# Lo parts of weights and V from GpSimd to VectorE, and the softmax's small scalings from ScalarE to GpSimd

## The chip, the cores and the metric

The kernel runs on one core of one Trainium2 chip. The core has TensorE (PE; its weight loads are listed apart as PEld), VectorE (DVE), ScalarE (ACT), GpSimd (POOL) and SyncE (SP, which here only issues DMAs). Each engine works through its own queue in order, and semaphores let one wait for another. The metric is the device time of one execution in microseconds (us); lower is better. Times of the kernel before are the median of three runs, and one more execution was recorded by the hardware profiler.

## The reference

Attention with a mask from hashing, followed by a feed-forward layer with ELU. Cut to what matters:

```python
# q, k, v: (4, 8, 768, 64); proj: (64, 6); w_in: (512, 2048); w_out: (2048, 512), all float32
q_bits = einsum('bhsd,dk->bhsk', q, proj) > 0      # 6 bits: a bucket per row
k_bits = einsum('bhsd,dk->bhsk', k, proj) > 0
mask = q_bucket[..., :, None] == k_bucket[..., None, :]
scores = where(mask, q @ k.T / sqrt(64), -1e9)
scores -= scores.max(-1)
attn = exp(scores)
attn = attn / (attn.sum(-1) + 1e-9)
x = (attn @ v), heads beside each other            # (3072, 512)
h = x @ w_in
g = where(h > 0, h, exp(min(h, 0)) - 1)
out = g @ w_out                                    # (3072, 512)
```

## The kernel before

**Numbers as two halves.** Matmuls run in f16. To keep precision each f32 operand is scaled by a power of two and split: the hi part is the scaled value rounded to f16, the lo part is the scaled value less the hi part, again in f16. A product is then three matmuls: hi by hi, hi by lo, lo by hi. The helper `scaled` makes a hi part, `rest` a lo part; each takes a `kind` and looks in the table ENGINES for the engine. An entry has two strings, the first for the time until all weights are decoded (`now[0]` is 0), the second for the time after; several letters in a string are used in turn. A is ScalarE, V is VectorE, G is GpSimd. For V, `rest` is one instruction on VectorE (L151, scalar_tensor_tensor: x times s, less hi). For G it is two on GpSimd: x times s in place (L153), then less hi (L154).

**Attention.** A batch has 8 heads in 4 pairs, and its 768 rows are cut into two chunks of three tiles of 128, so there are 8 chunks. A slot is one tile of rows of one head; 24 slots make a chunk, 192 the whole. In a slot PE computes the scores of 128 rows against 768 keys into a bank pair of PSUM (L556). The mask is part of this product: the bits are further rows of its operands. DVE copies the scores to SBUF as `pt` and takes each row's maximum into `m` (L568). Two slots make a duo. For a duo, `exps` multiplies the two columns of maxima by the row's factor into `nb` (L581), and ACT takes the exponentials with `nb` as bias and gives the row sums `sm` (L584). One slot later `splits` makes `r` from `sm`: times 2^-14, plus a small constant (L593), and DVE takes the reciprocal (L594). Then ACT makes the hi part of the duo's two `pt` tiles (L142, hl), DVE the lo part (L151, hl), and SP issues a DMA that transposes both into PT (L599). The product with V (`attend`, L607) follows AV_LAG = 4 slots after a pair's last slot and gives x16 in two halves (L616 on ACT, L617 on DVE).

**Preparation.** K and Q of coming pairs are loaded, scaled, split and transposed ahead of their slots. V of a batch is split by `prep_v`: its hi parts on ACT, its lo parts in 8 pieces of 128x384 per batch. For the first batch this happens while weights are still being decoded.

**Weights.** w_in and w_out come as 16 blocks of 128x512 each. Their f32 values are rebuilt from the two halves in which they are loaded: L516 on ACT, L517 and L518 on DVE; PE sums their squares (L526). Once a matrix's scale is known, `wsplit` makes a block's hi part on ACT (L142, W) and its lo part by `rest`. A block group (4 blocks of w_in, 4 of w_out) must be split before the feed-forward part reaches it (`need_w`).

**Feed-forward (MoE in the code).** It begins after slot 30 with chunk 0 and then runs beside the attention of later chunks. For each of 16 column blocks: 12 matmuls give h (L636); ACT takes the exponential (L647); POOL multiplies and adds (L650); DVE takes a maximum and a minimum (L651); ACT and DVE make hi and lo parts of g (L142 and L151, U); PE adds to the output banks (L672). At a chunk's end ACT and DVE empty three output banks and POOL issues the output DMA for each (L686).

**Order.** A planner sets the order within each engine's queue: it takes the program's order as priority and places what is ready by its own timing of the instructions. From the slot where the feed-forward part begins, PE's order is that of the program. An instruction that the planner put in a queue keeps the ones behind it waiting when its inputs are late.

Of the kernel before, what the change touches and what calls it, by code (L numbers as in the profile page):

```python
# [13 lines left out]
AF = mybir.ActivationFunctionType  # L14
ALU = mybir.AluOpType
# [7 lines left out]
P_TOP = 14  # L23
# [28 lines left out]
    "n_hi": ("A", "A"),  # L52
    "n_lo": ("V", "V"),
    "v_hi": ("A", "A"),
    "v_lo": ("G", "V"),
    "w_hi": ("A", "A"),
    "w_lo": ("G", "G"),
    "g_hi": ("A", "A"),
    "g_lo": ("V", "V"),
    "dup": ("V", "V"),  # L60
# [5 lines left out]
def lsh_attention_moe(  # L66
# [10 lines left out]
    nc = tc.nc  # L77
# [60 lines left out]
    def scaled(kind, o, x, s):  # L138

        e = engine(kind)  # L140
        if e == "A":
            nc.scalar.activation(o, x, AF.Copy, scale=s)  # L142
        elif e == "V":
            nc.vector.tensor_scalar(o, x, s, None, ALU.mult)
        else:
            nc.gpsimd.tensor_scalar(o, x, s, 1.0, ALU.mult, ALU.mult)

    def rest(kind, o, x, s, hi):

        if engine(kind) == "V":  # L150
            nc.vector.scalar_tensor_tensor(o, x, s, hi, ALU.mult, ALU.subtract)  # L151
        else:
            nc.gpsimd.tensor_scalar(x, x, s, 1.0, ALU.mult, ALU.mult)  # L153
            nc.gpsimd.tensor_tensor(o, x, hi, ALU.subtract)  # L154
# [421 lines left out]
    def exps(st, duo):  # L576

        m, pts = duo[0], duo[1:]
        w = len(pts)
        nb = small.tile([P, 2], F32, tag="nb", name="nb")  # L580
        nc.scalar.activation(nb[:, :w], m[:, :w], AF.Copy, scale=st["sg"][:, 1:2])  # L581
        sm = small.tile([P, 2], F32, tag="sm", name="sm")
        for n, pt in enumerate(pts):
            nc.scalar.activation(  # L584
                pt, pt, AF.Exp, bias=nb[:, n : n + 1], scale=st["sg"][:, 0:1], accum_out=sm[:, n : n + 1]
            )
        return sm, pts

    def splits(sm, pts, PTs):

        w = len(pts)
        r = small.tile([P, 2], F32, tag="r", name="r")
        nc.scalar.activation(r[:, :w], sm[:, :w], AF.Copy, scale=2.0**-P_TOP, bias=1e-9 * 2.0**-P_TOP)  # L593
        nc.vector.reciprocal(r[:, :w], r[:, :w])  # L594
        for n, pt in enumerate(pts):
            hl = pp.tile([P, 2, S], F16, tag="p", name="hl")
            scaled("p_hi", hl[:, 0, :], pt, r[:, n : n + 1])
            rest("p_lo", hl[:, 1, :], pt, r[:, n : n + 1], hl[:, 0, :])
            nc.sync.dma_start_transpose(PTs[n].rearrange("p x c e -> p (x c) e"), hl.rearrange("p x e -> p (x e)"))  # L599
# [189 lines left out]
    for ns in groups:  # L789
# [3 lines left out]
        for n in ns:  # L793
            at = lead[2] if early else begin[n] - PREP[2]

            w = 2 * chunks[pairs[n][0]]["nc"]
# [144 lines left out]
    def run_splits():  # L941
        if behind:
            splits(*behind.pop())

    for G in range(starts[-2] + 1):
        if G == starts[0]:
            ordered.enter_context(tc.manual_schedule(engines={mybir.EngineType.PE}))
        if G < len(slots):
            n, at = slots[G]
            c = chunks[pairs[n][0]]  # L950
            b, p, j, t = c["b"], pairs[n][1], at // c["nc"], at % c["nc"]
            now[0] = int(w_at == NSI + NSO)
            if t == 0:
                (PT,) = pt_ring.take(c["nc"], pairs[n][0])
                PTs = PTs + [PT] if j else [PT]
            if G < starts[0] and G % 2:
                s_tile = ps_o.tile([P, 2, 512], F32, tag="o", name="so")
            else:
                s_tile = ps_s.tile([P, 2, 512], F32, tag="s", name="s")
            scores(ks[b, p], qs[n], at, j, s_tile, duo, G >= starts[0])  # L960
            into.append(PT[:, t])

            run_splits()
            if len(into) == 2:
                behind.append((*exps(qs[n], duo), into))
                duo, into = [], []
            if at == 2 * c["nc"] - 1:
                assert not into
                waiting.append((G + AV_LAG, (n, PTs)))
        else:  # L970
            run_splits()
# [39 lines left out]
```

## Time and profile before

| | |
|---|---|
| median of 3 runs | 927.86 us (924.74 to 927.88) |
| profiled execution, its own time | 925.77 us |
| its span in the profile | 923.3 us |
| mean granted PE clock | 0.938 |
| GpSimd L650, L154, L153 | 128, 40 and 40 instructions |
| DMA moved | 135.11 MB, mean 146 GB/s |

The page of the profile gives each engine's busy time and its share of the span, and, for the costliest groups, a line of the kernel, engine, operation, the tiles written and read, shapes, the count, then busy us and mean ns of one; behind the last bar stands how long the engine sat idle just before them and what ended that. A row of waits reads: engine and line that waited, what it waited for, us in total, times, longest us. A row of one line's or tile's instructions gives minimum, median and maximum of the duration in ns, then the first and last start in us.

### The profile page before, as it was taken

The page shows a single profiled execution, that of the slowest core. Times are in us where ns is not written, and L with a number is a line of the kernel's source. Part 1 is how long each engine was busy: PE and PEld are TensorE (multiplying, and loading weights), DVE is VectorE, ACT ScalarE, POOL GpSimd, SP SyncE. Part 2 cuts the span into 40 slices and gives each one's busy share as a digit, 9 for nine tenths or more (in the row PEclk, how much of TensorE's full clock was granted, in tenths as well). Part 3 has the DMA queues.
Part 4 walks back from the last instruction along what each step waited for, and adds up shares of the span by engine and source line. Part 5 has one row for each costly group of instructions (what it writes and reads, how often), then busy time and mean ns, then how long its engine had stood idle before and what let it go on. Part 6 is the DMA issues. An engine that isn't in the chain of part 4 may idle for free.

```text
span 923.3 us, 14935 instructions
## 1 busy us (share of the span) xinstructions
PE 823.7 (89%) x5161; PEld 434.4 (47%) x5161; DVE 698.3 (76%) x1490; ACT 696.0 (75%) x1361; POOL 221.9 (24%) x259
## 2 busy tenths in 40 slices
PE   4475745899999999999989999999999999999996
PEld 2232312455545555555545555555445555555553
DVE  6999968788878778788868687889878687674332
ACT  7876878989869677789879677888687777774322
POOL 1703579631112011212211111221111112111211
PEclk9577656899999999999999999999999999999998
DMA  9799576798787857698897776896876678554000
GB/s 327 202 282 254 143 148 128 138 170 174 154 177 160 144 111 142 146 191 141 154 216 130 129 127 120 165 192 110 158 140 130 118 118 151 100 108 84 35 1 34
DMA packets 391338, 135.11 MB, mean 146 GB/s; under 512 B 368000, under 2 KB 385632, under 8 KB 391264
## 3 DMA queue, kind: packets, MB, share of 16 engines
q1 hardware_dynamic: 389184, 127.88, 69.3%
q0 software_dynamic: 1920, 6.29, 2.0%
q8 instruction: 40, 0.66, 0.3%
q14 instruction: 34, 0.28, 0.1%
q10 hardware_dynamic: 160, 0.00, 0.0%
HBM read 35.65 MB, written 6.29 MB: 45 GB/s over the span
## 4 chain that ended last, share of the span: by engine, by line
PE 45%; DVE 19%; DMA 13%; ACT 12%; issue 8%; POOL 1%; SPq 1%; ACTq 0%; POOLq 0%; DVEq 0%
PE h L636 16%; PE o L672 15%; PE s L556 7%; PE av L607 6%; DVE pt L568 5%; DVE hl L151 4%; DMA K<-natk 4%; ACT pt L584 3%; DMA O<-nat1q 3%; ACT hl L142 3%; DMA PT<-hl 2%; DMA out_dram<-W 2%; DVE W L518 1%; ACT U L647 1%; PE z L315 1%
## 5 line engine op out<-in xcount | busy, mean ns | idle before, releaser
L672 PE MATMUL o<-W,U 128*128 128x512 f16 x1152 | 280.9, 380 | 2.4 <-ACT W L142 2.4
L636 PE MATMUL h<-x,W 128*128 128x384 f16 x1536 | 280.5, 327 | 2.6 <-DVE x L617 2.2
L650 POOL TENSOR_SCALAR U<-U,ch 128x384 f32<-128x384 f32 x128 | 113.4, 886 | 572.1 <-ACT U L647 506.0
L636 PEld LDWEIGHTS <-W 128*128 128x128 f16 x1536 | 147.5, 98 | 114.1 <-issue 10.7
L151 DVE SCALAR_TENSOR_TENSOR hl<-pt,r,hl 128x768 f16<-128x768 f32 x192 | 193.9, 1038 | 6.3 <-ACT hl L142 5.9
L584 ACT ACTIVATE pt<-pt,nb,sg 128x768 f32<-128x768 f32 x192 | 195.3, 1018 | 2.2
L142 ACT ACTIVATE hl<-pt,r 128x768 f16<-128x768 f32 x192 | 168.4, 925 | 29.8 <-DVE r L594 27.6
L568 DVE TENSOR_SCALAR_CACHE_REDUCE pt<-s 128x768 f32<-128x768 f32 x177 | 168.0, 949 | 25.1 <-PE s L556 24.4
L556 PE MATMUL s<-K,O 128*128 128x384 f16 x708 | 151.5, 337 | 22.7 <-DVE pt L568 19.8
L672 PEld LDWEIGHTS <-U 128*128 128x128 f16 x1152 | 111.1, 98 | 122.3 <-issue 8.8
L556 PEld LDWEIGHTS <-O 128*128 128x128 f16 (+1 forms) x768 | 74.8, 102 | 115.6 <-issue 59.2
L651 DVE SCALAR_TENSOR_TENSOR U<-h,U 128x384 f32<-128x384 f32 x128 | 70.8, 553 | 74.8 <-POOL U L650 74.7
L647 ACT ACTIVATE U<-h,ch 128x384 f32<-128x384 f32 x128 | 72.8, 569 | 66.2 <-PE h L636 66.1
L607 PE MATMUL av<-PT,vhl 128*64 128x384 f16 x1152 | 106.9, 332 | 3.8 <-DMA PT<-hl 3.7
L151 DVE SCALAR_TENSOR_TENSOR U<-U,ch 128x384 f16<-128x384 f32 x128 | 79.6, 623 | 39.7 <-ACT U L142 39.4
L142 ACT ACTIVATE U<-U,ch 128x384 f16<-128x384 f32 x128 | 77.2, 605 | 40.8 <-DVE U L651 40.5
L607 PEld LDWEIGHTS <-vhl 128*64 128x64 f16 x1152 | 68.8, 111 | 44.4 <-issue 15.4
L154 POOL TENSOR_TENSOR W<-W 128x512 f16<-128x512 f32 x32 | 43.5, 1363 | 2.2
L581 ACT ACTIVATE nb<-m,sg 128x2 f32<-128x2 f32 x96 | 27.5, 287 | 16.4 <-DVE pt L568 15.9
L584 ACT ACTIVATION_READ_ACCUMULATOR pt<-pt,nb,sg 128x1 f32 x192 | 36.0, 187 | 0.0
L526 PE MATMUL acc<-W 128*128 128x128 bf16 x128 | 17.8, 283 | 19.7 <-DVE W L518 19.2
L556 PE MATMUL so<-K,O 128*128 128x384 f16 (+1 forms) x60 | 18.7, 449 | 17.9 <-DVE pt L568 16.6
(126 smaller groups left out, 632.5 us busy)
## 6 DMA issues: line engine op xcount, KB each, us to landing
U<-in_moe_w_in_dram SPq DMA_DIRECT2D x12, 512.0 KB
vf<-in_v_dram SPq DMA_DIRECT2D x16, 384.0 KB
U<-in_moe_w_out_dram SPq DMA_DIRECT2D x12, 512.0 KB
out_dram<-W POOLq DMA_DIRECT2D x24, 256.0 KB, 3.4
qst<-in_q_dram SPq DMA_DIRECT2D x30, 192.0 KB
kst<-in_k_dram SPq DMA_DIRECT2D x14, 384.0 KB
PT<-hl SPq DMA_TRANSPOSE x192
W<-in_moe_w_in_dram SPq DMA_DIRECT2D x4, 512.0 KB
```

Of the source, the lines that this page charges most:

```text
L142: nc.scalar.activation(o, x, AF.Copy, scale=s)
L151: nc.vector.scalar_tensor_tensor(o, x, s, hi, ALU.mult, ALU.subtract)
L154: nc.gpsimd.tensor_tensor(o, x, hi, ALU.subtract)
L556: nc.tensor.matmul(s_tile[:, n, :HALF], st[o][:rows, at, :], kst[kk][:rows, j * NC + n * HC : j * NC + (n + 1) * HC, :].rearrange("p a b - ...
L568: top = nc.vector.tensor_scalar(pt.rearrange("p (n e) -> p n e", n=2), s_tile[:, :, :HALF], CLAMP, None, ALU.max, ALU.max, accum_out=duo[0 ...
L584: nc.scalar.activation(pt, pt, AF.Exp, bias=nb[:, n : n + 1], scale=st["sg"][:, 0:1], accum_out=sm[:, n : n + 1])
L607: nc.tensor.matmul(av[j * D : (j + 1) * D], vt[:, j, c, vx, :], PTs[j][:, :, px, c, :], start=n == 0, stop=n == last,)
L636: nc.tensor.matmul(h, WH[:, g * KT + t, wx, fc * P : (fc + 1) * P], c["xs"][t][:, xx, :], start=n == 0, stop=n == 3 * KT - 1,)
L647: nc.scalar.activation(e, h, AF.Exp, scale=c["ch"])
L650: nc.gpsimd.tensor_scalar(e, e, c["up"], c["dn"], ALU.mult, ALU.add)
L651: nc.vector.scalar_tensor_tensor(e, h, 0.0, e, ALU.max, ALU.min)
L672: nc.tensor.matmul(o[t][:, :DO], g16[:, gx, t * P : (t + 1) * P], WH[:, NSI + 1 + f, wx, :], start=f == 0 and i == 0, stop=f == NF - 1 and ...
```

## The change

The lo parts of V in the first batch and of all weight blocks are made by VectorE instead of GpSimd, so `rest` takes its one-instruction form for them. The two small instructions per duo that make `nb` and the input of the reciprocal `r` are issued on GpSimd instead of ScalarE. Nothing else differs.

```diff
@@ ENGINES
     "v_hi": ("A", "A"),
-    "v_lo": ("G", "V"),
+    "v_lo": ("V", "V"),
     "w_hi": ("A", "A"),
-    "w_lo": ("G", "G"),
+    "w_lo": ("V", "V"),
@@ exps
-        nc.scalar.activation(nb[:, :w], m[:, :w], AF.Copy, scale=st["sg"][:, 1:2])
+        nc.gpsimd.tensor_scalar(nb[:, :w], m[:, :w], st["sg"][:, 1:2], 1.0, ALU.mult, ALU.mult)
@@ splits
-        nc.scalar.activation(r[:, :w], sm[:, :w], AF.Copy, scale=2.0**-P_TOP, bias=1e-9 * 2.0**-P_TOP)
+        nc.gpsimd.tensor_scalar(r[:, :w], sm[:, :w], 2.0**-P_TOP, 1e-9 * 2.0**-P_TOP, ALU.mult, ALU.add)
         nc.vector.reciprocal(r[:, :w], r[:, :w])
```

## The prediction

> **What bounds the kernel now.** I read the page's busy times first, then busy times by stage, then who waited for whom, then groups by line.
>
> ```profile
> span 923.3 us, 14935 instructions
> PE   823.7 (89%) x5161; PEld 434.4 (47%) x5161; DVE 698.3 (76%) x1490; ACT 696.0 (75%) x1361; POOL 221.9 (24%) x259
> PE 45%; DVE 19%; DMA 13%; ACT 12%; issue 8%; POOL 1%; SPq 1%; ACTq 0%; POOLq 0%; DVEq 0%
> ```
>
> PE is busy 89% of the span and 45% of the chain that ended last. But that is an average over two kinds of stage. The next rows are windows: from:to and length in us, then busy us (with counts) of PE, PEld, DVE, ACT, POOL, then granted clock, DMA share and GB/s.
>
> ```profile
> 28.00:48.00 20.00, 6.63 (x43) 3.99 (x42) 19.86 (x39) 15.52 (x28) 17.85 (x16) 0.50 0.75 197
> 48.00:81.00 33.00, 24.70 (x162) 11.99 (x163) 31.43 (x69) 24.07 (x44) 0.00 (x0) 0.81 1.02 263
> 81.00:119.00 38.00, 24.68 (x148) 12.87 (x147) 37.27 (x82) 32.49 (x62) 23.57 (x18) 0.62 0.66 166
> 119.00:170.00 51.00, 27.18 (x141) 11.69 (x140) 37.58 (x63) 42.71 (x86) 40.77 (x38) 0.63 0.78 149
> 170.00:200.00 30.00, 28.58 (x175) 14.88 (x174) 23.91 (x56) 26.25 (x51) 15.76 (x16) 0.94 0.77 133
> 200.00:835.00 635.00, 618.07 (x3973) 329.12 (x3970) 502.21 (x1066) 505.00 (x1003) 104.90 (x121) 1.00 0.77 146
> ```
>
> From 28 to 119 us DVE is the bound: 19.86 of 20, 31.43 of 33, 37.27 of 38 us (DMA is full too from 48 to 81, share 1.02). From 119 to 170 nothing is full: ACT 84%, POOL 80%, DVE 74%, and the end wanders between them and DMAs. From 200 on, PE is the bound: 618.07 of 635 us at full granted clock. All that can be won there is 16.9 us of PE idle time.
>
> **Part 1: lo parts of V and of the weights from POOL to DVE.** POOL loses two instructions per lo part (multiply L153, subtract L154); DVE gets one scalar_tensor_tensor (L151). DVE's cost for 512 columns isn't in the trace; two neighbours of the same operation are.
>
> ```profile
> L151 DVE SCALAR_TENSOR_TENSOR vhl<-vf,vs,vhl 128x384 f16<-128x384 f32 x24 | 13.9, 608 | 1.2 <-ACT vhl L142 1.2
> L151 DVE SCALAR_TENSOR_TENSOR natk<-kst,ks,natk 128x768 f16<-128x768 f32 x11 | 11.1, 1009 | 0.2
> ```
>
> (1009 - 608)/384 is 1.04 ns a column, so 512 columns cost 608 + 128 x 1.04 = 0.742 us; the two rows bound it. DVE gains 32 x 0.742 = 23.7 us for the weights and 8 x 0.608 = 4.9 us for the first batch's V. Against this stands what POOL's work does to DVE today. Same forms by window, 28 to 48 us (POOL busy), 48 to 81 (POOL idle), 81 to 119, 119 to 192:
>
> ```profile
> L518 DVE SCALAR_TENSOR_TENSOR W<-U,W 128x512 int32<-128x512 int32 x5 | 5.0, 1010 | 0.1
> L517 DVE TENSOR_SCALAR W<-W 128x512 int32<-128x512 int32 x6 | 4.6, 773 | 0.0
> L151 DVE SCALAR_TENSOR_TENSOR W<-W,ks 128x768 f16<-128x768 f32 x2 | 3.0, 1498 | 0.0
> ...
> L518 DVE SCALAR_TENSOR_TENSOR W<-U,W 128x512 int32<-128x512 int32 x9 | 6.2, 686 | 0.1
> L151 DVE SCALAR_TENSOR_TENSOR hl<-pt,r,hl 128x768 f16<-128x768 f32 x6 | 5.8, 1015 | 0.0
> L517 DVE TENSOR_SCALAR W<-W 128x512 int32<-128x512 int32 x12 | 4.9, 417 | 0.9 <-ACT W L516 0.8
> ...
> L151 DVE SCALAR_TENSOR_TENSOR hl<-pt,r,hl 128x768 f16<-128x768 f32 x6 | 6.8, 1154 | 0.0
> L517 DVE TENSOR_SCALAR W<-W 128x512 int32<-128x512 int32 x9 | 5.4, 620 | 0.0
> L518 DVE SCALAR_TENSOR_TENSOR W<-W 128x512 int32<-128x512 int32 x2 | 2.6, 1280 | 0.0
> ...
> L151 DVE SCALAR_TENSOR_TENSOR hl<-pt,r,hl 128x768 f16<-128x768 f32 x20 | 23.3, 1202 | 0.3 <-ACT hl L142 0.3
> L594 DVE RECIPROCAL r<-r 128x2 f32<-128x2 f32 x9 | 1.4, 158 | 6.8 <-ACT r L593 6.7
> ```
>
> Where POOL multiplies and subtracts, DVE's instructions are stretched; that goes with the work. Stage by stage:
> 28 to 48 us: +4.9; back come 5 x (1010-686) = 1.6, 6 x (773-417) = 2.1 and 2 x (1498-1009) = 1.0 us. Net +0.2.
> 81 to 119: POOL's 18 instructions are 9 lo parts, +6.7; back come 6 x (1154-1015) = 0.8, 9 x (620-417) = 1.8 and 2 x (1280-686) = 1.2. Net +2.9, all on the path, since DVE is full.
> 119 to 192: the other 23 lo parts, +17.1; back come 20 x (1202-1015) = 3.7 us and most of the 6.7 us in which DVE waits for r (part 2). Net +6.7 us, into a stage where DVE has 13.4 us idle up to 170 us and 6 more by 200; I take 0 on the path. The cover is that idle time, and the planner's freedom: a group's parts are wanted only when MoE reaches its blocks. Gone, it costs 6.7 us.
> 170 to 200: PE now waits once for a lo part from POOL as MoE starts.
>
> ```profile
> PEld L636 <- POOL W L153: 2.4, 1, 2.4
> ```
>
> This wait goes: DVE has a part done 0.742 us after its hi part. PE idles 1.4 us in that window, so I count -1.4 and not -2.4. Sum of part 1: 0.2 + 2.9 + 0 - 1.4 = **+1.7 us**.
>
> **Part 2: nb and r from ACT to POOL.** Per duo ACT loses one of each:
>
> ```profile
> L581 ACT ACTIVATE nb<-m,sg 128x2 f32<-128x2 f32 x96 | 27.5, 287 | 16.4 <-DVE pt L568 15.9
> L593 ACT ACTIVATE r<-sm 128x2 f32<-128x2 f32 x96 | 18.3, 190 | 0.2
> ...
> L153 POOL TENSOR_SCALAR W<-W,w1s x16: 687/698/1659, 115.0 to 188.2; 128x512 f32<-128x512 f32 x16
> L153 POOL TENSOR_SCALAR vf<-vf,vs x8: 582/945/1532, 29.2 to 42.9; 128x384 f32<-128x384 f32 x8
> ...
> L650 POOL TENSOR_SCALAR U<-U,ch x128: 652/666/2766, 172.9 to 910.4; 128x384 f32<-128x384 f32 x128
> L650 POOL TENSOR_SCALAR U<-U,ch 128x384 f32<-128x384 f32 x128 | 113.4, 886 | 572.1 <-ACT U L647 506.0 <-ACT r L593 64.9 <-PE z L315 1.2
> ...
> 410.41 0.19 ACT L584 ACTIVATION_READ_ACCUMULATOR pt<-pt,nb,sg 128x1 f32 x1
> 412.69 0.19 ACT L593 ACTIVATE r<-sm 128x2 f32<-128x2 f32 x1
> ```
>
> ACT is freed of 0.477 us a duo. A two-column instruction on POOL isn't in the trace. From the minima, (687-582)/128 = 0.82 ns a column, so 582 - 382 x 0.82 = 0.27 us is an estimate for two columns. L650's mean lies 0.23 us above its minimum: POOL is held up by others. I take 0.27 + 0.23 = 0.50 us each, 1.0 us a duo, 0.52 more than ACT. Ends: 0 below; above, each held through a whole DVE hl (1.01 us), 1.28 us, +2.1 us a duo. But r leaves ACT's queue: in the two timeline rows sm was there at 410.60 and r ran at 412.69, 2.1 us later, since ACT did other work first. So I count the longer duration as paid by the shorter queue: 0. At the upper end half of the 15 duos before MoE would show it, 7.5 x 2.1 = 16 us. After, the lag of 4 slots (two duos) before the AV product hides it.
>
> Before 170 us: 20 hl from 119 to 192 us are 10 duos, so some 7 fall into 119 to 170: 3.3 us less on ACT, which is 84% full; half on the path: **-1.7**. After 200 us, PE's idle time by 100 us:
>
> ```profile
> 200.00:300.00 100.00, 97.45 (x632) 51.93 (x628) 84.25 (x184) 85.58 (x173) 19.95 (x19) 0.98 0.84 171
> 300.00:400.00 100.00, 98.16 (x630) 52.24 (x623) 76.42 (x163) 76.83 (x153) 13.91 (x19) 1.00 0.74 137
> 400.00:500.00 100.00, 95.36 (x625) 49.97 (x623) 82.38 (x182) 84.47 (x172) 19.25 (x19) 1.00 0.87 169
> 500.00:600.00 100.00, 96.79 (x616) 51.89 (x614) 75.34 (x162) 75.81 (x152) 14.20 (x19) 1.00 0.75 136
> 600.00:700.00 100.00, 95.31 (x618) 50.24 (x616) 82.33 (x182) 80.23 (x160) 18.36 (x19) 1.00 0.79 150
> 700.00:800.00 100.00, 100.00 (x638) 53.61 (x636) 76.92 (x154) 76.58 (x150) 14.98 (x20) 1.00 0.70 128
> ```
>
> The windows with a new batch's K and V (first, third, fifth) have ACT at 83.4 on average and 11.9 us of PE idle in all; the others 76.4 and 5.1. Twelve duos a window (156 hl, or 78 duos, in 635 us by a row below) give ACT back 5.7 us, 0.81 of the 7.0 us between the kinds. If PE's idle time follows, 0.81 x (11.9 - 5.1) = 5.5 us go: **-5.5**. What is late next is the K transposes' DMA, which this leaves alone.
>
> The added waits: an Exp on ACT waits for POOL's nb, and behind it in ACT's queue stand MoE's Exp and hi parts; the reciprocal on DVE waits for POOL's r, and behind it stand the row maxima that free the score bank for PE. No SP transfer is moved, but POOL issues the 24 output DMAs, which now queue with nb and r; at 0.50 us each and an output wait off the path I count 0.
>
> One rule stands against this. The Trainium skill, "SBUF — State Buffer", section "Who interferes with whom", says that GpSimd and a DVE instruction with two SBUF inputs exclude each other for a whole instruction, whichever started first. By that rule the trace agrees for POOL's long work (L518 at 1010 against 686 ns); it would also let nb and r hold up DVE, which is the second rival below, 929 us by its rows, where I count nothing.
>
> **Sum:** +1.7 - 1.7 - 5.5 = -5.5 us. The profiled execution took 925.77 us (span 923.3 and 2.5 around it): 920.3. The median before is 927.86, 2.1 above; on its scale I forecast **922.4 us**.
>
> **The rivals.**
> Nothing comes of it: from 200 us PE idles for transfers, not for ACT, and the start is even: 925 to 930, 927. For: DMA runs at 0.84, 0.87 and 0.79 in exactly the windows with most idle time. Against: ACT is fullest there too.
> POOL holds up DVE. The row for hl over 200 to 835 us:
>
> ```profile
> L151 DVE SCALAR_TENSOR_TENSOR hl<-pt,r,hl 128x768 f16<-128x768 f32 x156 | 153.5, 1010 | 5.9 <-ACT hl L142 5.7
> ```
>
> nb and r bring 192 x 0.27 = 52 us of POOL work, and hl runs 153.5 of 635 us, 24%; 12.5 us of delay to hl if each meeting holds it, half on the path: +6, 929. Against: POOL works 104.9 us in this stage, and hl takes 1010 ns, as long as with POOL idle (1015).
> POOL's queue becomes the bound (slower): at a chunk's end an output DMA on POOL waits for its evacuation, and nb behind it keeps ACT's Exp, then DVE and the score bank.
>
> ```profile
> POOL out_dram L686 <- ACT W L142: 14.8, 8, 4.8
> POOL out_dram L686 <- ACT nb L581: 12.5, 6, 2.3
> ```
>
> 27.3 us over 14 waits is 1.95 us; if PE idles for one at each of 8 ends, +15.6: 938. It decides once the delay is more than the lag of two duos leaves. Against: nb could be planned ahead of the DMA.
> DVE becomes the bound from 81 to 192 us (slower): all 32 lo parts land where DVE is waited for: 23.7 less the 7.5 us of stretch that goes is 16.2 instead of 2.9, +13.3: 936. Against: DVE's idle 13.4 us from 119 on.
>
> **How the numbers follow.** Faster as summed 0.42; nothing 0.25; POOL holds DVE 0.08; POOL's queue 0.13; DVE bound 0.12. About 0.5%, 4.6 us, is what can be told here from no change, so faster is below 923.2 and slower above 932.5: the first case is faster, the next two are the same, the last two slower: 0.42, 0.33, 0.25. The forecast lies near the edge of the first; its own range is 911 to 926. Low end: all 16.9 us of PE idle after 200 us gone instead of 5.5, **911**. High end: the two slower cases and the upper end of POOL's small instructions (922.4 + 16): **938**. About 0.15 is left out.
>
> **What would show it.** Right: hl near 1.01 us from 81 to 192 us, r's wait on DVE gone, MoE's first POOL instruction (L650) no later than 172.9 us, less PE idle in the three heavy windows. Wrong: ACT or DVE waiting long for POOL's nb or r; L650 starting later; POOL's small instructions near 1 us.

## The result and the profile after

The changed kernel takes 931.96 us (median of 8 runs, 929.45 to 933.93) against 926.34 us of the kernel before (8 runs beside them, 923.84 to 927.88). The ratio is 1.0059, 95% interval 1.0047 to 1.0071: slower by 5.5 us (0.0059 of 926.34), where 5.5 us faster was forecast. The profiled execution took 930.52 us, its span is 928.7.

From the page of the changed kernel: the span, the busy times, and groups (line, engine, operation, tiles, count, then busy us and mean ns of one, then idle time before them and what ended it):

```profile
span 928.7 us, 15031 instructions
PE 826.9 (89%) x5161; PEld 434.9 (47%) x5161; DVE 709.7 (76%) x1530; ACT 662.7 (71%) x1169; POOL 202.0 (22%) x371
L584 ACT ACTIVATE pt<-pt,nb,sg 128x768 f32<-128x768 f32 x192 | 195.4, 1018 | 72.4 <-POOL nb L581 71.9
...
L581 POOL TENSOR_SCALAR nb<-m,sg 128x2 f32<-128x2 f32 x96 | 54.9, 572 | 289.8 <-DVE pt L568 182.1
...
L593 POOL TENSOR_SCALAR r<-sm 128x2 f32<-128x2 f32 x96 | 21.7, 226 | 193.6 <-ACT pt L584 193.6
L594 DVE RECIPROCAL r<-r 128x2 f32<-128x2 f32 x96 | 15.7, 164 | 56.7 <-POOL r L593 56.1
```

ScalarE lost 33.3 us of work (696.0 to 662.7) and got 71.9 us of idle time at the exponential in its place: there it stands for GpSimd's nb. VectorE stands 56.1 us at the reciprocal for r (24.2 us before).

Where in time? Windows of the changed kernel (from:to and length, busy us with counts of PE, PEld, DVE, ACT, POOL, then granted clock, DMA share, GB/s):

```profile
28.00:48.00 20.00, 6.47 (x37) 3.57 (x36) 19.83 (x59) 17.64 (x32) 2.34 (x5) 0.50 0.78 213
...
81.00:119.00 38.00, 21.01 (x101) 9.94 (x100) 33.02 (x77) 31.90 (x59) 5.21 (x8) 0.55 0.71 195
119.00:170.00 51.00, 34.06 (x186) 18.35 (x185) 46.55 (x104) 40.25 (x69) 5.84 (x12) 0.67 0.74 135
...
200.00:835.00 635.00, 613.54 (x3951) 324.05 (x3950) 508.52 (x1066) 476.62 (x847) 157.14 (x275) 1.00 0.76 145
200.00:300.00 100.00, 95.54 (x623) 50.65 (x622) 85.88 (x183) 81.19 (x149) 27.69 (x43) 1.00 0.86 172
300.00:400.00 100.00, 100.00 (x643) 52.90 (x642) 79.72 (x168) 73.94 (x131) 23.41 (x45) 1.00 0.72 137
400.00:500.00 100.00, 92.18 (x589) 47.44 (x587) 80.33 (x173) 76.64 (x141) 26.18 (x41) 0.98 0.85 167
500.00:600.00 100.00, 99.38 (x639) 52.44 (x637) 79.10 (x168) 73.65 (x130) 21.95 (x45) 1.00 0.74 136
600.00:700.00 100.00, 92.78 (x602) 49.42 (x601) 81.84 (x180) 75.24 (x135) 28.80 (x43) 1.00 0.79 149
```

Up to 200 us nothing is lost; MoE's first L650 starts at 172.6 us (172.9 before). From 200 to 835 us PE is busy 613.54 instead of 618.07 us, 4.5 us less, and the loss sits in the three windows with a new batch: 95.54, 92.18 and 92.78 where 97.45, 95.36 and 95.31 stood. These are the windows in which the forecast saw PE win.

Which wait of PE is it? From 200 to 835 us the matmul of the scores waits longer for its bank, which VectorE's maximum frees (waits: engine and line, what for, us in total, times, longest); first the kernel before, then the changed one:

```profile
PE s L556 <- DVE pt L568: 10.5, 10, 2.3
...
PE s L556 <- DVE pt L568: 15.8, 13, 2.3
```

That is 5.3 us more. PE's other waits in this stage cancel: for ScalarE's emptying of an output bank 3.6 us instead of 2.4, for the transposed tiles before the AV product 0.2 us instead of 2.4. Why the maximum is late shows on VectorE: in 9 of the 13 waits, 10.9 of 15.8 us, its longest idle time in the 5 us ahead of that maximum was at the reciprocal, waiting for r (before: 2 waits, 0.6 us). r needs the row sums, the sums need the exponential, and the exponential waits for nb.

How one wait comes about is seen in the timeline (start us, us, engine, line, operation, tiles; in brackets the idle time before it and what ended that). The 47th duo's second maximum and what follows it, kernel before:

```profile
430.53 0.95 DVE L568 TENSOR_SCALAR_CACHE_REDUCE pt<-s 128x768 f32<-128x768 f32 x1
430.90 1.75 ACT L142 ACTIVATE hl<-pt,r 128x768 f16<-128x768 f32 x2
...
431.41 0.08 DVE L568 DVE_READ_ACCUMULATOR pt<-s 128x1 f32 x1
...
432.55 0.56 ACT L647 ACTIVATE U<-h,ch 128x384 f32<-128x384 f32 x1
...
433.02 0.28 ACT L581 ACTIVATE nb<-m,sg 128x2 f32<-128x2 f32 x1
...
433.33 1.03 ACT L584 ACTIVATE pt<-pt,nb,sg 128x768 f32<-128x768 f32 x1
```

and the same duo in the changed kernel:

```profile
432.36 0.94 DVE L568 TENSOR_SCALAR_CACHE_REDUCE pt<-s 128x768 f32<-128x768 f32 x1
...
433.24 0.07 DVE L568 DVE_READ_ACCUMULATOR pt<-s 128x1 f32 x1
433.24 1.94 DVE L151 SCALAR_TENSOR_TENSOR hl<-pt,r,hl 128x768 f16<-128x768 f32 x2
433.28 1.11 ACT L142 ACTIVATE vhl<-vf,vs 128x384 f16<-128x384 f32 x2
433.48 1.75 POOL L581 TENSOR_SCALAR nb<-m,sg 128x2 f32<-128x2 f32 x1 [2.51 <-DVE pt L568]
...
435.26 1.03 ACT L584 ACTIVATE pt<-pt,nb,sg 128x768 f32<-128x768 f32 x1 [0.87 <-POOL nb L581]
```

Before, ScalarE used the 1.5 us after the maximum for other work, made nb in 0.28 us and went on without a gap. Now GpSimd starts nb 0.17 us after the maximum, but VectorE has begun its two lo parts, nb lasts until they end (1.75 us), and ScalarE stands 0.87 us at the exponential with everything behind it in its queue.

The small instructions' own rows (minimum, median, maximum ns, then first and last start):

```profile
L581 POOL TENSOR_SCALAR nb<-m,sg x96: 260/490/1802, 25.6 to 838.1; 128x2 f32<-128x2 f32 x96
...
L593 POOL TENSOR_SCALAR r<-sm x96: 181/191/1289, 28.3 to 840.6; 128x2 f32<-128x2 f32 x96
```

Sorted by the VectorE instruction that runs as nb begins, nb takes 0.26 us beside none (13 cases) and beside L651, which reads one of its inputs from PSUM (14 cases), but 1.08 us in the mean beside hl's lo part, which reads two tiles in SBUF (27 cases). In 18 of these 27 it ends 0.13 us after that lo part; in 8 it stays through VectorE's next two-input instruction as well, though nb had begun before that one, as in the timeline above (1.75 us). The Trainium skill, "SBUF — State Buffer", section "Who interferes with whom", says this: a VectorE instruction with two SBUF inputs and a GpSimd instruction that reads SBUF shut each other out. The trace agrees. But that the one begun first also goes first, as the forecast put it, doesn't hold in those 8 cases, as far as the recorded starts tell. The forecast had weighed this page with the holding the other way round (the holding of GpSimd stood only at the upper end of its duration, 1.28 us each); hl's lo part is not held up, at 1013 ns in the mean of the run now and 1010 before (from 200 us on).

### The profile page after: what moved, and what is told of

Read it like the earlier page. It is cut to its first block, busy times and chain, and to the rows that moved or that the text cites. A ratio compares the mean times of both kernels' runs of the same rounds, so it can differ in the third digit from the quotient of the medians.

```text
span 928.7 us, 15031 instructions
## 1 busy us (share of the span) xinstructions
PE 826.9 (89%) x5161; PEld 434.9 (47%) x5161; DVE 709.7 (76%) x1530; ACT 662.7 (71%) x1169; POOL 202.0 (22%) x371
## 5 line engine op out<-in xcount | busy, mean ns | idle before, releaser
L584 ACT ACTIVATE pt<-pt,nb,sg 128x768 f32<-128x768 f32 x192 | 195.4, 1018 | 72.4 <-POOL nb L581 71.9
L151 DVE SCALAR_TENSOR_TENSOR hl<-pt,r,hl 128x768 f16<-128x768 f32 x192 | 188.7, 1013 | 7.1 <-ACT hl L142 6.8
L556 PE MATMUL s<-K,O 128*128 128x384 f16 x708 | 152.4, 338 | 27.7 <-DVE pt L568 25.7
L650 POOL TENSOR_SCALAR U<-U,ch 128x384 f32<-128x384 f32 x128 | 109.7, 857 | 213.2 <-ACT U L647 207.7
L651 DVE SCALAR_TENSOR_TENSOR U<-h,U 128x384 f32<-128x384 f32 x128 | 70.8, 553 | 71.8 <-POOL U L650 71.2
L581 POOL TENSOR_SCALAR nb<-m,sg 128x2 f32<-128x2 f32 x96 | 54.9, 572 | 289.8 <-DVE pt L568 182.1
L142 ACT ACTIVATE U<-U,ch 128x384 f16<-128x384 f32 x128 | 77.2, 604 | 29.6 <-DVE U L651 29.5
L593 POOL TENSOR_SCALAR r<-sm 128x2 f32<-128x2 f32 x96 | 21.7, 226 | 193.6 <-ACT pt L584 193.6
L594 DVE RECIPROCAL r<-r 128x2 f32<-128x2 f32 x96 | 15.7, 164 | 56.7 <-POOL r L593 56.1
L526 PE MATMUL acc<-W 128*128 128x128 bf16 x128 | 17.3, 280 | 22.4 <-DVE W L518 14.8
```

The costliest lines, as they stand in the source:

```text
L556: nc.tensor.matmul(s_tile[:, n, :HALF], st[o][:rows, at, :], kst[kk][:rows, j * NC + n * HC : j * NC + (n + 1) * HC, :].rearrange("p a b - ...
L581: nc.gpsimd.tensor_scalar(nb[:, :w], m[:, :w], st["sg"][:, 1:2], 1.0, ALU.mult, ALU.mult)
L584: nc.scalar.activation(pt, pt, AF.Exp, bias=nb[:, n : n + 1], scale=st["sg"][:, 0:1], accum_out=sm[:, n : n + 1])
L650: nc.gpsimd.tensor_scalar(e, e, c["up"], c["dn"], ALU.mult, ALU.add)
L651: nc.vector.scalar_tensor_tensor(e, h, 0.0, e, ALU.max, ALU.min)
```

## The experiments

Where the expectations give theories letters, they are: D, VectorE's added load; R, r on GpSimd; N, nb off ScalarE; L, GpSimd's instruction shut out by VectorE's; Q, ScalarE's queue standing whichever engine makes nb; W, the later theory: ScalarE's relief is worth little, and the wait for a nb that comes later is what costs, by its length. Ratios are to the kernel before on the same chip.

| run | nb on | r on | lo parts on | ratio (95%) |
|---|---|---|---|---|
| the change | GpSimd | GpSimd | VectorE | 1.0059 (1.0047 to 1.0071) |
| e1_lo_only | ScalarE | ScalarE | VectorE | 0.9963 (0.9945 to 0.9981) |
| e2_small_only | GpSimd | GpSimd | GpSimd | 1.0139 (1.0108 to 1.0170) |
| e3_lo_nb | GpSimd | ScalarE | VectorE | 1.0185 (1.0154 to 1.0216) |
| e4_lo_r | ScalarE | GpSimd | VectorE | 0.9980 (0.9958 to 1.0002) |
| e5_nb_dve | VectorE | ScalarE | VectorE | 1.0155 (1.0132 to 1.0178) |
| e6_both_dve | VectorE | VectorE | VectorE | 1.0155 (1.0130 to 1.0180) |
| e7_nb_dve_r_pool | VectorE | GpSimd | VectorE | 1.0134 (1.0110 to 1.0158) |
| e8_nb_pool_twice | GpSimd, in two steps | ScalarE | VectorE | 1.0334 (1.0312 to 1.0355) |
| e9_lo_idle_pool | ScalarE, GpSimd's unread | ScalarE | VectorE | 0.9990 (0.9974 to 1.0006) |
| e10_pool_idle_act | GpSimd, ScalarE's unread | ScalarE | VectorE | 1.0270 (1.0252 to 1.0289) |
| e11_nb_pool_first | GpSimd, high priority | ScalarE | VectorE | 1.0203 (1.0180 to 1.0225) |
| e12_r_unscaled | ScalarE | not scaled | VectorE | 1.0040 (1.0022 to 1.0059) |
| e14_no_nb | once, at the start | ScalarE | VectorE | 0.9972 (0.9960 to 0.9985) |
| e15_nb_pool_unread | GpSimd, unread | ScalarE | VectorE | 0.9946 (0.9926 to 0.9966) |
| e16_after_nb_unread | GpSimd, unread | GpSimd | VectorE | 0.9911 (0.9888 to 0.9935) |

**The parts by themselves.** e1 undoes part 2, e2 undoes part 1:

```diff
 e1, against the changed kernel
-        nc.gpsimd.tensor_scalar(nb[:, :w], m[:, :w], st["sg"][:, 1:2], 1.0, ALU.mult, ALU.mult)
+        nc.scalar.activation(nb[:, :w], m[:, :w], AF.Copy, scale=st["sg"][:, 1:2])
...
-        nc.gpsimd.tensor_scalar(r[:, :w], sm[:, :w], 2.0**-P_TOP, 1e-9 * 2.0**-P_TOP, ALU.mult, ALU.add)
+        nc.scalar.activation(r[:, :w], sm[:, :w], AF.Copy, scale=2.0**-P_TOP, bias=1e-9 * 2.0**-P_TOP)
 e2, against the changed kernel
-    "v_lo": ("V", "V"),
+    "v_lo": ("G", "V"),
-    "w_lo": ("V", "V"),
+    "w_lo": ("G", "G"),
```

> Part 1 alone: lo parts of V and weights on DVE, nb and r stay on ACT. Theory N (nb on POOL costs the time: ACT waits 71.9 us for it in the changed kernel, where before it waited 15.9 us for the maxima) and theory R (r on POOL costs it: DVE waits 56.1 us at the reciprocal instead of 24.2) both expect no loss here: 0.995 to 1.002, since MoE's first exponential came at the same time in both kernels (171.9 against 172.3 us). Theory D (DVE's extra 28 us) expects all of the change's loss here, 1.005 to 1.007.

> Part 2 alone: nb and r on POOL, the lo parts stay on POOL as well. Theories N and R expect at least the change's loss, 1.005 or more; up to 1.015 because nb and r now also queue behind the 40 lo parts on POOL up to 190 us, and MoE starts later than 172 us. Theory D expects 1.000 or less.

Measured: 0.9963 and 1.0139. Part 1 alone is faster than either kernel, part 2 alone is slower than both parts together: the loss is all in part 2, and D falls. In e2 nb also queues behind the lo parts on GpSimd, and MoE's first exponential starts at 177.8 us instead of 172.25.

**nb or r.** e3 leaves only nb on GpSimd, e4 only r; each takes one of e1's two edits back:

```diff
 e3, against e1
-        nc.scalar.activation(nb[:, :w], m[:, :w], AF.Copy, scale=st["sg"][:, 1:2])
+        nc.gpsimd.tensor_scalar(nb[:, :w], m[:, :w], st["sg"][:, 1:2], 1.0, ALU.mult, ALU.mult)
 e4, against e1
-        nc.scalar.activation(r[:, :w], sm[:, :w], AF.Copy, scale=2.0**-P_TOP, bias=1e-9 * 2.0**-P_TOP)
+        nc.gpsimd.tensor_scalar(r[:, :w], sm[:, :w], 2.0**-P_TOP, 1e-9 * 2.0**-P_TOP, ALU.mult, ALU.add)
```

> Part 1 and nb on POOL; r back on ACT. Theory N expects the whole loss, 1.005 to 1.007, with ACT waiting some 70 us for nb and DVE waiting 20 to 25 us for r as before. Theory R expects 0.998 to 1.001.

> Part 1 and r on POOL; nb back on ACT. Theory R expects the whole loss, 1.005 to 1.007, with DVE waiting 50 us or more at the reciprocal. Theory N expects 0.998 to 1.001 and little waiting of ACT for nb's inputs (about 16 us).

Measured: 1.0185 and 0.9980. e3 loses some three times what N expected. r on GpSimd is even with part 1 alone, although VectorE waits for it in e4 too (waits: engine and line, what for, us in total, times, longest):

```profile
DVE r L594 <- POOL r L593: 43.6, 44, 2.3
```

So R falls: that wait is covered. In e3 the waits and the stage from 200 us read

```profile
ACT pt L584 <- POOL nb L581: 72.3, 55, 2.5
```

```profile
200.00:835.00 635.00, 607.76 (x3877) 319.70 (x3875) 493.70 (x1051) 476.60 (x909) 140.86 (x195) 0.99 0.75 144
```

that is, the wait of the whole change, and PE busy 10.3 us less than before (618.07). MoE's first exponential comes at 176.0 us, 4.2 later than in part 1 alone. To see what the 72.3 us are, I took each duo's gap on ScalarE from 172 us on, from the end of the instruction ahead (nb not counted as one) to the duo's first exponential, and cut it at the end of the maximum. Over 81 duos part 1 alone stands 13.6 us until the maximum and 17.8 us after it (nb's own run is in that); e3 20.9 and 45.2 us; the whole change 25.4 and 40.9 us. (The expectation of e14 has 29.6 and 63.5 us for the sums of the first two, 1.9 and 2.6 us less than this count.) The most of what is added comes after the maximum: nb's way through GpSimd.

The standing alone doesn't set the price, though: e3 and the whole change stand equally long, 66.1 and 66.3 us, yet e3 is 12 us slower (1.0185 against 1.0059). With r left on ScalarE, behind the exponentials that stand, PE waits 8.5 us in 8 times for the transposed tiles before the AV product from 200 to 835 us, where the whole change has 0.2 us; 4.1 us more lie before MoE's first exponential. No run separates r's place from the order that came with it.

**nb on VectorE.** If L were all, nb right behind the maximum on VectorE itself would be free of it:

```diff
 e5, against e1
-        nc.scalar.activation(nb[:, :w], m[:, :w], AF.Copy, scale=st["sg"][:, 1:2])
+        nc.vector.tensor_scalar(nb[:, :w], m[:, :w], st["sg"][:, 1:2], None, ALU.mult)
 e6, against e5
-        nc.scalar.activation(r[:, :w], sm[:, :w], AF.Copy, scale=2.0**-P_TOP, bias=1e-9 * 2.0**-P_TOP)
+        nc.vector.tensor_scalar(r[:, :w], sm[:, :w], 2.0**-P_TOP, 1e-9 * 2.0**-P_TOP, ALU.mult, ALU.add)
 e7, against e5
-        nc.scalar.activation(r[:, :w], sm[:, :w], AF.Copy, scale=2.0**-P_TOP, bias=1e-9 * 2.0**-P_TOP)
+        nc.gpsimd.tensor_scalar(r[:, :w], sm[:, :w], 2.0**-P_TOP, 1e-9 * 2.0**-P_TOP, ALU.mult, ALU.add)
```

> Part 1, nb on DVE, r on ACT: nb leaves ACT as in the changed kernel, but does not go to POOL. Theory L (nb on POOL is held until DVE's running two-input instruction ends, and ACT stands still at the Exp behind it) expects no loss: 0.990 to 1.000, ACT's wait for nb under 30 us in all instead of 72. Theory Q (nb anywhere off ACT makes ACT stand still, since the Exp is queued ahead of other work) expects 1.010 or more and some 60 us or more of waiting.

> Part 1, nb and r's scaling both on DVE. Theory L expects 0.988 to 1.000: ACT is freed of 45.8 us of work, DVE takes some 96 x 0.3 = 29 us. Theory Q expects 1.005 or more.

> Part 1, nb on DVE, r on POOL: the changed kernel with nb alone moved from POOL to DVE. Theory L expects the whole loss to go: 0.990 to 1.000. Theory Q expects 1.004 to 1.008 as in the changed kernel.

Measured: 1.0155, 1.0155, 1.0134, so L alone doesn't explain the loss. Q misses too: its 60 us of waiting in e5 were 38.9, and e7 is above its 1.004 to 1.008. nb itself takes 0.22 us on VectorE, but other VectorE work is queued between the maximum and nb (none in only 9 of 96 duos of e5): from the maximum's end to the exponential it is, after 172 us, 1.47 us in the median of e5 and 1.69 of e7, 1.10 in e3 and 0.58 in part 1 alone. In e5, 9 us are lost before MoE begins (first exponential at 180.9 us), so its 38.9 us of waiting for nb don't stand for its whole loss.

**The wait made longer.** nb in two chained GpSimd steps:

```diff
 e8, against e3
-        nc.gpsimd.tensor_scalar(nb[:, :w], m[:, :w], st["sg"][:, 1:2], 1.0, ALU.mult, ALU.mult)
+        half = small.tile([P, 2], F32, tag="half", name="half")
+        nc.gpsimd.tensor_scalar(half[:, :w], m[:, :w], st["sg"][:, 1:2], 1.0, ALU.mult, ALU.mult)
+        nc.gpsimd.tensor_scalar(nb[:, :w], half[:, :w], 1.0, 1.0, ALU.mult, ALU.mult)
```

> Part 1, nb on POOL in two chained instructions (the second multiplies by one), r on ACT: the suspected cost doubled. With one instruction the ratio was 1.0185 and ACT waited 72 us. Theory L expects at least 0.26 us more of waiting per duo, 25 us or more in all, and a ratio of 1.025 to 1.045. Theory Q expects the ratio to stay, 1.014 to 1.022, since the planner counts the second instruction and puts other work ahead of the Exp.

Measured: 1.0334. By the gaps worked out as above, standing after the maximum goes from 45.2 to 62.5 us, 17.3 more (L expected 25 or more), and the span from 940.8 to 955.4 us, 14.6 more. The wait list and the stage from 200 us:

```profile
ACT pt L586 <- POOL nb L583: 89.1, 57, 3.3
...
PE s L556 <- DVE pt L568: 45.4, 40, 4.3
```

```profile
200.00:835.00 635.00, 591.04 (x3772) 313.93 (x3772) 481.63 (x1029) 465.49 (x885) 174.88 (x264) 1.00 0.74 140
```

The second row shows where it reaches PE: the score bank is freed by VectorE's maximum, which stands in VectorE's queue, often behind an instruction that waits for a result of ScalarE. In the same view of the whole change that wait of PE is 25.7 us in 24 times, of part 1 alone 20.4 in 21.

**GpSimd's presence, ScalarE's relief, the place in the queue.** Three kernels, each with one of them alone (in the first two, one statement a line here):

```diff
 e9, against e1 (ScalarE's nb is read, GpSimd's nj is not)
+        nj = small.tile([P, 2], F32, tag="nj", name="nj")
+        nc.gpsimd.tensor_scalar(nj[:, :w], m[:, :w], st["sg"][:, 1:2], 1.0, ALU.mult, ALU.mult)
 e10, against e3 (GpSimd's nb is read, ScalarE's nj is not)
+        nj = small.tile([P, 2], F32, tag="nj", name="nj")
+        nc.scalar.activation(nj[:, :w], m[:, :w], AF.Copy, scale=st["sg"][:, 1:2])
 e11, against e3 (nb and both exponentials)
+        with tc.high_priority():
```

> Part 1 with nb and r on ScalarE as before, and GpSimd making the same nb a second time into a tile that nothing reads (96 extra GpSimd operations, fed by the same maximum at the same place). ScalarE's, VectorE's and TensorE's orders are those of part 1 alone. If what costs is that a GpSimd operation runs there at all (it meets VectorE's two-input operations and lasts 0.9 us beside them), this is like nb on GpSimd with r on ScalarE: 1.015 to 1.019. If what costs is only that the exponential waits for its result (theory W), this is like part 1 alone: 0.995 to 0.999.

> Part 1 with nb on GpSimd and read by the exponential, and ScalarE still making it too, at its old place, into a tile that nothing reads: ScalarE has no relief, and its order is closer to that of part 1 alone. Theory W (ScalarE stands at the exponential for a result that comes later, whatever it is spared): 1.015 to 1.025, and the profile shows ScalarE's waits for GpSimd's nb again, some 30 to 50 us. A rival (the planner's new order, made for a ScalarE without nb, is what costs): 0.997 to 1.008.

> Part 1 with nb on GpSimd, r on ScalarE, and both nb and the exponentials given high priority in the planner, so that they stand as early as they can. Theory W: no gain, since the wait is for a result and not for a place: 1.012 to 1.025. The rival (order): it moves by more than 0.8% against the same kernel without the priority (1.0185), in either direction.

Measured: 0.9990, 1.0270, 1.0203. e9 has e1's orders and GpSimd's instruction at its place, met by VectorE's lo parts as often (33 of 96, 1.12 us in the mean); it is 0.3% behind part 1 alone, which the two intervals hardly tell from nothing, where nb read from GpSimd costs 2.2%. Its presence is not the loss. e10 lies above the 1.015 to 1.025 of W, with 25.2 us of waiting for nb (30 to 50 expected): with the wait kept, 0.85% goes with ScalarE's relief being taken back. e11 shows that an earlier place for nb and the exponential doesn't help; other changes of the order it leaves untested.

**Relief without a new wait.** e12 drops r's scale and its counterpart after the AV product; e14 makes nb once:

```diff
 e12, against e1
-        nc.scalar.activation(r[:, :w], sm[:, :w], AF.Copy, scale=2.0**-P_TOP, bias=1e-9 * 2.0**-P_TOP)
-        nc.vector.reciprocal(r[:, :w], r[:, :w])
+        nc.vector.reciprocal(r[:, :w], sm[:, :w])
...
-        f = 2.0**-P_TOP
+        f = 1.0
 e14, against e1
-        nb = small.tile([P, 2], F32, tag="nb", name="nb")
-        nc.scalar.activation(nb[:, :w], m[:, :w], AF.Copy, scale=st["sg"][:, 1:2])
+        if not kept: kept.append(const.tile([P, 2], F32, name="nb")); nc.scalar.activation(kept[0], m, AF.Copy, scale=st["sg"][:, 1:2])
+        nb = kept[0]
```

> Part 1, nb on ScalarE, and no scale of the row sums at all: the reciprocal is taken of the sums themselves, and the factor 2^-14 is left out of the AV product's copy too (f = 1.0), so the result is the same up to rounding. ScalarE loses r (0.19 us a duo, 18.3 us in all) and nothing waits for another engine in its place. The prediction's step (TensorE's idle time in the heavy windows follows ScalarE's load) gives 0.19/0.477 of (5.5 + 1.7) us, 2.9 us below part 1 alone: 0.993. The rival (ScalarE's load is not what those windows wait for, relief is worth nothing): 0.995 to 0.999, as part 1 alone.

> Part 1, r on ScalarE, and nb made once, from the first duo, and used for every duo: the bias of each later duo is left out. ScalarE loses 95 of 96 nb (0.289 us each, 27.5 us in all), and no exponential waits for a maximum's accumulator through nb. The prediction's step gives 0.289/0.477 of 7.2 us, 4.4 us below part 1 alone: 0.9915. Theory W: ScalarE's standing for nb (29.6 us after the MoE's start in part 1 alone, 63.5 with nb on GpSimd) goes too; going by 19.2 us of span for 33.9 us of standing, up to 16 us more: 0.975 to 0.990. The rival (neither ScalarE's load nor its standing is what decides, but the planner's order, which moves here as much as in the slow kernels): 0.995 or above.

Measured: 1.0040 and 0.9972. Both miss what W and the forecast's step gave. With nb gone from ScalarE, e14 is only even with part 1 alone. Its exponential still waits for the maximum, whose instruction writes pt:

```profile
ACT pt L584 <- DVE pt L568: 26.6, 43, 2.0
```

so ScalarE still stands for maxima, as W had not reckoned; that 27.5 us of work less on ScalarE bring nothing is what it shows. e12 is 0.8% slower than part 1 alone although it has less work and no new wait, the instructions of ScalarE and VectorE last as long in both from 200 us on, and the mean granted clock over all executions is the same (0.939 and 0.940); the planner laid out the queues anew, and which place of that order costs was not found. It sets a scale: by order alone, as far as is seen, a kernel here may move by 0.8%, 7 us.

**The dependence alone.** The sharpest pair: GpSimd makes nb for each duo as in e3 and in the whole change, but nothing waits for it.

```diff
 e15, against e3; e16, against the changed kernel
-        nb = small.tile([P, 2], F32, tag="nb", name="nb")
+        nb = small.tile([P, 2], F32, tag="nb", name="nb") if kept else const.tile([P, 2], F32, name="nb0")
-        nc.gpsimd.tensor_scalar(nb[:, :w], m[:, :w], st["sg"][:, 1:2], 1.0, ALU.mult, ALU.mult)
+        nc.gpsimd.tensor_scalar(nb[:, :w], m[:, :w], st["sg"][:, 1:2], 1.0, ALU.mult, ALU.mult); kept.append(nb); nb = kept[0]
```

> Part 1 with nb on GpSimd and r on ScalarE, as in the run that took 1.0185, but every exponential reads the first duo's nb: GpSimd still makes nb for every duo, and nothing reads it. Left out: each later duo's own bias. Theory W (the wait for GpSimd's result is what costs; ScalarE's relief is worth nothing): 0.994 to 1.004. The rival (GpSimd's small operations beside VectorE, or nb's absence from ScalarE with the order that the planner then makes): 1.012 to 1.019.

> The whole change, with the same edit: GpSimd makes nb and r, r is read, and every exponential reads the first duo's nb. Left out: each later duo's own bias. Theory W: 0.994 to 1.003, as part 1 with r on GpSimd (0.998). The rival (what the change loses is not in the wait for nb): 1.004 to 1.008, as the whole change.

Measured: 0.9946 against e3's 1.0185, and 0.9911 against the change's 1.0059: 22.1 and 13.7 us of 926.3 go with the dependence, 3.4 and 2.4 us either way by the intervals. e16 is better than W's 0.994 to 1.003. GpSimd still runs all 96 and r, as e16's rows of nb and of the waits show, and PE is busy 622.32 us from 200 to 835:

```profile
L581 POOL TENSOR_SCALAR nb<-m,sg x96: 252/263/2696, 25.6 to 826.6; 128x2 f32<-128x2 f32 x96
```

```profile
POOL r L593 <- ACT pt L584: 76.4, 86, 5.4
```

```profile
200.00:835.00 635.00, 622.32 (x3999) 327.12 (x3997) 511.11 (x1071) 483.90 (x852) 148.10 (x280) 1.00 0.77 147
```

Against 613.54 in the change that is 8.8 us of PE's time in this stage alone.

The edit takes a second thing away: nb needs both maxima of a duo; without it the first exponential needs only its own, and starts, in the median from 172 us on, 2.8 us before the second maximum's end in e16, 1.0 us after it in the change. e14 has the same freedom (2.7 us before it) and is even with part 1 alone, so this by itself shows no gain.

What this pair can't part is the wait and the order that the planner makes for it; both go with the dependence, and 13.7 us is about twice what order alone moved in e12. Two things speak for the wait, without proving it: every kernel whose exponential reads a nb of another engine (nine of them, the change among them) lies at 1.0059 or above, every one that doesn't at 1.0040 or below; and e8's longer wait costs nearly its length. e3 and the change with their equal standing show that the rest of the order sets what a wait costs.

e16 is no version to keep: a bias common to a row cancels in the softmax, but the first duo's maxima don't keep other rows in the exponential's range. Of the kernels that leave nothing out, part 1 alone has the lowest ratio, faster than both the kernel before and the changed one; e4 lies within its interval.

## Why the prediction was wrong

**The step that failed** is the one on the added waits. The term stood at nothing. The forecast named the wait ("an Exp on ACT waits for POOL's nb, and behind it in ACT's queue stand MoE's Exp and hi parts") and had counted it away under part 2: "I count the longer duration as paid by the shorter queue: 0", and after the start "the lag of 4 slots (two duos) before the AV product hides it". The duration was not the point. The estimate of 1.0 us for nb and r together was too high if anything (572 + 226 ns in the mean, 0.80 us). But the shorter queue is r's, and r on GpSimd alone was neutral (0.9980). nb's own queue got no shorter: before, ScalarE made nb when it came to it and ran on; now nb is done when GpSimd is let in.

And the lag covers the AV product alone: there PE waits 0.2 us from 200 to 835 us. It doesn't cover the other path, which the forecast named as well ("the reciprocal on DVE waits for POOL's r, and behind it stand the row maxima that free the score bank for PE"): the late exponential makes r late, VectorE stands at the reciprocal (56.1 us), and the score bank comes free late (PE's wait of 15.8 instead of 10.5 us). By e16 the term was 13.7 us and not 0, with the order that goes with it. The forecast's own signs of being wrong said as much: long waits of ScalarE for nb and of VectorE for r came; a later L650 and small GpSimd instructions near 1 us in the mean didn't.

**The 5.5 us of ScalarE's relief after 200 us** were no gain in the change: PE lost 4.5 us in that stage. Relief of nb alone gave nothing (e14). With both gone from ScalarE and nothing waiting for nb, e16 is 4.8 us below part 1 alone (0.9911 against 0.9963; 2.7 us either way by the two intervals), not far from the 7.2 us that the two relief terms (1.7 and 5.5) make. But that is less than the 7 us that order alone moved in e12, and r's relief alone gave nothing either (e4). Whether the term had the right size stays open; the change doesn't show it.

**Part 1** was put at +1.7 us and measured -3.4 us (0.9963; -5.1 to -1.8 by the interval). The price was right, 0.742 us forecast and 0.744 measured; the stretch went as forecast. Wrong was "all on the path, since DVE is full" for 81 to 119 us. The row of part 1 alone for that stage, and its lo parts in it:

```profile
81.00:119.00 38.00, 22.02 (x138) 11.78 (x133) 32.14 (x83) 33.77 (x65) 0.00 (x0) 0.60 0.70 182
```

```profile
L151 DVE SCALAR_TENSOR_TENSOR W<-W,w0s 128x512 f16<-128x512 f32 x7 | 5.2, 746 | 0.0
```

VectorE, 37.27 us busy there before, is busy 32.14 with 7 lo parts added: other work of that stage fell elsewhere, and a full engine in one window was not a bound that stays. Where the 3.4 us come from the trace doesn't settle; the profiled span gives 1.7 of them, 0.4 before MoE's first exponential, and 0.6 lie outside the span (an execution of the kernel before is 2.4 us longer than its span, of part 1 alone 1.8).

**The 1.7 us before 170 us** came to little: MoE's first exponential starts at 171.9 us in the change, 171.8 in part 1 alone.

**The rivals.** Nothing comes of it: no. POOL holds DVE: the exclusion is there, but hl's lo part stays at 1013 ns; it's nb that is held. POOL's queue at the output DMAs: its point was nb held up before ScalarE's Exp, then VectorE and the score bank, and that is what happened, but not behind a DMA at 8 chunk ends: behind VectorE's lo parts, and along the whole heavy windows. Its price, 938, was too high for the change and its place wrong. DVE the bound from 81 to 192 us: no, MoE starts no later. The time lies within the range (911 to 938) only because the range took in the slower rivals, of which POOL's queue named the path with another cause; slower by over 0.5% had been given 0.25.

## What to carry to other kernels

Before moving a tiny instruction off a busy in-order engine, look who reads it: if the same engine does, it had been free of waiting there, and afterwards the engine stands at the reader, with all that is queued behind. Count such a wait from the producer's end to the reader, with what the new engine has queued or holds, and not from the instruction's own 0.2 to 0.3 us. Then test the move with the dependence taken away; the difference is the price of the wait together with the order that goes with it, here 13.7 us.

## What was not expected of the hardware

A two-column GpSimd instruction, 0.26 us by itself, lasted 1.08 us in the mean when it began beside VectorE's 128x768 instruction with two SBUF inputs (27 of 96 cases), and up to 1.80 us, when VectorE began a second two-input instruction ahead of it; beside L651, with one SBUF input, it kept its 0.26 us in all 14 cases. In e3 it met that instruction in 38 of 96 cases, 40%, where the instruction ran in 24% of the time from 200 to 835 us before the change: fed by VectorE's maximum, nb begins just as VectorE takes up what is next.
